# A second load buffer for stage D, and stages A and B one round earlier

## The chip, the cores and the metric

The kernel runs on one core of a Trainium2 chip. The metric is device time in microseconds (us) of one execution.

## The reference

```python
# x: [8, 3008, 256]; w_r, w_i: [256, 256]; w_in: [256, 2048]; w_out: [2048, 256]
X = np.fft.rfft(x, axis=1)                  # along the 3008 positions
Yr = X.real @ w_r - X.imag @ w_i + b_r
Yi = X.real @ w_i + X.imag @ w_r + b_i
Yr = np.sign(Yr) * np.maximum(np.abs(Yr) - 0.01, 0.0)
Yi = np.sign(Yi) * np.maximum(np.abs(Yi) - 0.01, 0.0)
y = np.fft.irfft(Yr + 1j * Yi, n=3008, axis=1).reshape(24064, 256)
h = np.maximum(y @ w_in, 0.0)
out = h * h @ w_out                         # [24064, 256]
```

## The kernel before

Two jobs run interleaved on all engines: the transform of a batch (stages A to D) and the two matrix products on the tokens of the batch before it.

**Products.** The tokens of a batch are cut into six chunks (`WIDTHS`, one of 470, four of 508, one of 506), 48 chunks in all. A chunk takes eight *rounds* (`NU`), one for each pair of 128 of the 2048 hidden features, so a batch takes a *cycle* of 48 rounds and the kernel 384 rounds and two to drain. In round r, TensorE (PE) runs the first product `mm1` into `ph`; ScalarE (ACT) applies two ReLUs (`g<-ph`) and a square (`g<-g`); VectorE (DVE) makes three sums (`sums`, L858 to L860). In round r+1 ScalarE makes a high part `gh` and VectorE a low part `gl` of these seven tiles, and in round r+2 PE runs the second product `mm2` of seven block products into `po`. Each product is three matmuls (`mm3`: high by high, high by low, low by high, profile lines L205 to L207). `ph` has one buffer: `mm1` of round r+1 waits for the two ReLUs of round r. After the second round of the next chunk (rounds 1, 9, 17, ... of a cycle) `put_together` copies and combines `po` with one ScalarE and seven VectorE operations (L876, L878 to L884); VectorE runs these during the round that follows (rounds 2, 10, 18, ..., 42), and `mm2` of that round writes `po` anew.

**Transform.** Stage A (13 groups, `plan_a`) loads `xin`, folds it on VectorE (`f`, L233 and L234), makes `fh` and `fl`, multiplies by a small table (`psa`), evicts to `eva` on ScalarE (L670) and stores to scratch memory in DRAM. Stage B and C (12 pairs, one every three rounds, `plan_b`): a load `bin`, points `psb`, copy `x`, its high and low parts `xh` and `xl` (L708), the mix by the weights (`psm`), bias, threshold, a turned copy `z`, its parts `zh` and `zl`, the way back (`psc`), eviction `evc` (L750) and a store to a second scratch. Stage D (13 groups, `plan_d`): a load `din`, points `psd` (L290), a copy `dv`, an unfolding on VectorE (`dx`, L297 and L298), and a high and a low part (L798, L802) into `xt`, the input of `mm1`.

**Order.** Nothing is scheduled by the compiler. Each step of a stage is registered with `at(round, place, do)`, and a round runs its places in a fixed order: load, `gh`, a1, `mm1`, p1, ReLUs and square, `gl`, v1, sums, `mm2`, p2, a2, v2, put-together. Steps at the same place run in the order in which they were registered. `stage_b[b]` is the round in which stage B of batch b begins; stage A begins 15 rounds earlier (`TURN`); `done[b]` is 41 rounds later. Stage D takes rounds in which stage B runs its points (`pair_round`) or in which there is no stage B. Every batch has two places where two stage D groups stand in rounds next to each other: its first two groups (rounds 45 and 46 of a cycle) and its third and fourth.

**Buffers and queue.** All transfers are issued by SyncE (SP) in order; one that waits for a buffer or for data holds all behind it. `din` has one buffer, `zh` one, `ld` (for `xin` and `bin`) two, `ev` (for `eva` and `evc`) two, the PSUM tag `f` of all small products two.

Of the kernel before, what the change touches and what calls it, by code (L numbers as in the profile page):

```python
# [45 lines left out]
GROUPS = [(g, min(W, N2 - g)) for g in range(0, N2, W)]  # L46
# [15 lines left out]
NCH = len(WIDTHS)  # L62
# [94 lines left out]
NU = NF // 2  # L157
# [7 lines left out]
def fft_mix_moe(ctx: ExitStack, tc: tile.TileContext, xp, xu, w_r, w_i, b_r, b_i,  # L165
                w_in, w_out, t_u, t_a, t_b, t_b0, t_m, t_d, sgn, outT):
    nc = tc.nc
    B = xp.shape[0] + xu.shape[0]
# [90 lines left out]
    nch = NCH * B  # L259
# [4 lines left out]
    def pieces(b, i):  # L264

        g, w = GROUPS[i]
        a, z = b * S + N1 * g, b * S + N1 * (g + w)
        out = []
        for c in range(NCH * b, NCH * (b + 1)):
            lo, hi = max(a, col0[c]), min(z, col0[c] + cols[c])  # L270
            if lo < hi:
                out.append((c, lo - col0[c], hi - lo, lo - a))
        return out

    def alloc_x(c):
        return [const.tile([P, 2, NCOL], F32R, tag=f"xt{k}", name=f"xt{k}", bufs=2) for k in range(2)]

    def load_d(b, i, t):
        g, w = GROUPS[i]
        nc.sync.dma_start(out=t[:NR * w], in_=scr2[b][:, g:g + w, :])  # L280

    def points_d(i, t, ps):
        g, w = GROUPS[i]
        n = NR * w
        tab = 0 if w == W else 2
        ps = ps[:, :4 * n].rearrange("p (k c m) -> p k c m", k=2, c=2)
        for part in range(2):
            for k in range(2):
                s = part * D + k * P
                nc.tensor.matmul(ps[:, k, part], t[:n, s:s + P], tD[:n, tab + part, :n],  # L290
                                 start=True, stop=True)
        return ps

    def unfold(i, ps, v, xf):
        w = GROUPS[i][1]
        n, m = NR * w, N1 * w
        nc.vector.tensor_add(xf[:, :, :n], ps[:, :, 0], v[:, :, :n])  # L297
        nc.vector.tensor_sub(xf[:, :, n:m], ps[:, :, 0, w:], v[:, :, w:n])  # L298
# [318 lines left out]
    def tl(tag, shape=(P, 512), dt=F32, bufs=1, name=None):  # L617
        return sb.tile(list(shape), dt, tag=tag, name=name or tag, bufs=bufs)

    def pst(name):  # L620
        return ps_f.tile([P, 512], F32, tag="f", name=name)
# [9 lines left out]
    def at(r, place, do):  # L631
        plan.setdefault((r, place), []).append(do)
# [5 lines left out]
    def plan_a(b, r0):  # L638
        for i, (g, w) in enumerate(GROUPS):
            def steps(i=i, n=NR * w, tab=0 if w == W else 2):  # L640
                s = {}

                def load():
                    if i == 0:
                        scratch1(b)
                    s["t"] = tl("ld", bufs=2, name="xin")[:n]
                    load_x(b, i, s["t"])

                def folded():
                    s["f"] = tl("ft", name="f")[:n]  # L650
                    fold(s["f"], s["t"])

                def high():
                    s["h"] = tl("fh", dt=F32R)[:n]
                    nc.scalar.copy(s["h"], s["f"])

                def low():
                    s["l"] = tl("fl", dt=F32R)[:n]
                    nc.vector.tensor_sub(s["l"], s["f"], s["h"].bitcast(F32))

                def points():
                    s["o"] = pst("psa")[:n]
                    for c in range(2):
                        cs = slice(c * D, c * D + D)
                        mm3(s["o"][:, cs], (tAs[0][:n, tab + c, :n], tAs[1][:n, tab + c, :n]),
                            (s["h"][:, cs], s["l"][:, cs]), True, True)

                def out():
                    e = tl("ev", bufs=2, name="eva")[:n]
                    nc.scalar.copy(e, s["o"])  # L670
                    store_a(b, i, e)

                r = r0 + i
                at(r - 2, "load", load)
                at(r, "v1", folded)
                at(r, "a2", high)
                at(r, "v2", low)
                at(r + 1, "p2", points)
                at(*((r + 2, "a1") if i + 1 < len(GROUPS) else (r + 1, "a2")), out)

            steps()
# [86 lines left out]

            steps()

    def plan_d(b, i, r):
        s = {}
        parts = pieces(b, i)

        def load():
            s["t"] = tl("din")
            load_d(b, i, s["t"])

        def points():
            s["ps"] = points_d(i, s["t"], pst("psd"))  # L780

        def take():
            s["v"] = tl("xh", (P, 3, 2, P), name="dv").rearrange("p a b m -> p (a b m)")
            s["v"] = s["v"][:, :2 * NR * W].rearrange("p (k m) -> p k m", k=2)
            nc.scalar.copy(s["v"][:, :, :s["ps"].shape[3]], s["ps"][:, :, 1])

        def unfolded():
            if len(parts) == 1:
                x = tl("xl", (P, 3, 2, P), name="dx").rearrange("p a b m -> p (a b m)")
            else:  # L790
                x = tl("o0", (P, 2, HALF), name="dx").rearrange("p a m -> p (a m)")
            s["x"] = x[:, :2 * N1 * W].rearrange("p (k m) -> p k m", k=2)
            unfold(i, s["ps"], s["v"], s["x"])

        def high(c, to, m, a):
            if c not in xts:
                xts[c] = alloc_x(c)
            nc.scalar.copy(xts[c][0][:, :, to:to + m], s["x"][:, :, a:a + m])  # L798

        def low(c, to, m, a):  # L800
            hi, lo = (x[:, :, to:to + m] for x in xts[c])
            nc.vector.tensor_sub(lo, s["x"][:, :, a:a + m], hi.bitcast(F32))  # L802

        at(max(r - 2, done.get(b, 0)), "load", load)
        at(r, "p1", points)
        at(r, "a2", take)
        at(r, "v2", unfolded)
        for k, part in enumerate(parts):

            q = NU * (part[0] - 1) if k else r + 1  # L810
            at(q, "a1", lambda part=part: high(*part))
            at(q, "v1", lambda part=part: low(*part))

    stage_b = {b: 3 + NU * NCH * (b - 1) for b in range(1, B)}

    done = {b: r + PAIR * (NPAIR - 1) + 8 for b, r in stage_b.items()}

    def pair_round(r):

        return all((r - r0) % PAIR == 0 for r0 in stage_b.values() if r0 <= r < r0 + PAIR * NPAIR)  # L820

    for b, r in stage_b.items():
        if b > 1:
            plan_a(b, r - TURN)
        plan_b(b, r)
    for c in range(1, nch):
        b = c // NCH
        rounds = [r for r in range(max(NU * (c - 1) - 1, 2), NU * c - 1) if pair_round(r)]
        units = [i for i in range(len(GROUPS)) if pieces(b, i)[0][0] == c]
        for i, r in zip(units, rounds[-len(units):]):  # L830
            assert r - 1 >= done.get(b, 0), (c, i, r)
            assert len(pieces(b, i)) == 1 or r >= NU * (c - 1) + 2, (c, i, r)
            plan_d(b, i, r)

    def mm1(c, j):
        n = cols[c]
# [55 lines left out]
    last = nch * NU  # L892
    with tc.manual_schedule():
        for r in range(last + LAG):
            c, j = divmod(r, NU)
# [68 lines left out]
```

## Time and profile before

| | |
|---|---|
| time, median of 3 runs | 2669.49 us (2668.97 to 2671.93) |
| profiled execution: time, span | 2671.44 us, 2669.7 us |
| busy: PE, DVE, ACT | 2583.5 us (97%), 2123.1 us (80%), 2014.2 us (75%) |
| TensorE clock granted, mean | 0.991 |
| first round begins | 143.9 us |

A busy time is the sum over an engine's instructions; idle time is put down to what ended it ("<-"). SPq is SP's queue of transfers, PEld the loading of weights on PE, which runs beside its matmuls. The first cycle ends near 466 us, and cycles 1 to 5 take about 322 us each; cycle 6 has no stage A, cycle 7 only stage D and products.

### The profile page before, as it was taken

To read this page: it belongs to the slowest core of one execution; us is meant where nothing else is said; L and a number is where in the kernel's file an instruction comes from. 1 tells how busy PE (TensorE), PEld (TensorE's weight loads), DVE (VectorE), ACT (ScalarE), POOL (GpSimd) and SP (SyncE) were. 2 spreads that over 40 slices of the span, in tenths; PEclk is the share of its full clock that TensorE was granted. 3 is DMA by queue.
4 is the path that set the end of the run, shared out by engine and by line. 5 is a ranking of instruction groups with operands and counts; after the bars stand their busy time and mean duration, and the time that the engine had idled before them with its cause. 6 is when DMAs were issued, how large, how long until landed. Compare 5 with 4: busy or idle time off the path is not lost.

```text
span 2669.7 us, 42564 instructions
## 1 busy us (share of the span) xinstructions
PE 2583.5 (97%) x16760; PEld 2328.8 (87%) x16760; DVE 2123.1 (80%) x3177; ACT 2014.2 (75%) x2785; POOL 50.9 (2%) x60
## 2 busy tenths in 40 slices
PE   6879999999999999999999999999999999999998
PEld 3579998999989999899988999899998999998887
DVE  5768888888888888888887888878888888877776
ACT  3667887777877887777877787777787778776765
POOL 1410000000000000000000000000000000000000
PEclk8989999999999999999999999999999999999999
DMA  9611113111132112311122111221113111110000
GB/s 264 196 39 48 46 54 97 47 58 40 54 92 61 40 47 64 104 40 42 36 87 86 39 40 58 83 71 39 51 50 92 55 54 48 31 34 25 22 25 16
DMA packets 127753, 165.16 MB, mean 62 GB/s; under 512 B 11184, under 2 KB 89762, under 8 KB 127362
## 3 DMA queue, kind: packets, MB, share of 16 engines
q1 hardware_dynamic: 127554, 162.44, 20.5%
q8 instruction: 133, 2.18, 0.3%
q14 instruction: 66, 0.54, 0.1%
HBM read 87.43 MB, written 74.97 MB: 61 GB/s over the span
## 4 chain that ended last, share of the span: by engine, by line
PE 61%; DVE 19%; ACT 12%; DMA 4%; issue 3%; POOL 1%; ACTq 0%; SPq 0%; DVEq 0%; POOLq 0%
PE ph L205 8%; PE ph L206 8%; PE ph L207 8%; PE po L205 7%; PE po L207 7%; PE po L206 7%; ACT gh L901 6%; DVE gl L909 5%; DVE g L858 3%; PE psb L242 3%; PE psm L207 2%; PE psd L290 2%; PE psm L205 2%; PE psm L206 2%; ACT g L852 2%
## 5 line engine op out<-in xcount | busy, mean ns | idle before, releaser
L909 DVE TENSOR_TENSOR gl<-g,gh 128x1778 fp32r<-128x1778 f32 (+1 forms) x384 | 763.6, 1989 | 332.9 <-ACT gh L901 332.9
L901 ACT CAST gh<-g 128x1778 fp32r<-128x1778 f32 (+1 forms) x384 | 638.7, 1663 | 381.7 <-DVE g L860 305.8
L205 PE MATMUL po<-gh,wo 128*128 128x254 f32 (+1 forms) x2688 | 764.8, 285 | 6.4 <-DVE o L878 3.6
L206 PE MATMUL po<-gl,wo 128*128 128x254 f32 (+1 forms) x2688 | 753.0, 280 | 2.6 <-DVE gl L909 2.6
L207 PE MATMUL po<-gh,wo 128*128 128x254 f32 (+1 forms) x2688 | 752.9, 280 | 0.0
L205 PE MATMUL ph<-xt,wi 128*128 128x508 f32 (+2 forms) x1536 | 608.6, 396 | 16.2 <-ACT xt L199 10.6
L206 PE MATMUL ph<-xt,wi 128*128 128x508 f32 (+2 forms) x1536 | 599.9, 391 | 1.8 <-DVE xt L802 1.7
L207 PE MATMUL ph<-xt,wi 128*128 128x508 f32 (+2 forms) x1536 | 599.0, 390 | 0.0
L205 PEld LDWEIGHTS po<-gh,wo 128*128 128x128 f32 x2688 | 509.4, 190 | 21.1 <-DVE o L878 7.7
L206 PEld LDWEIGHTS po<-gl,wo 128*128 128x128 f32 x2688 | 509.8, 190 | 10.7 <-DVE gl L909 3.0
L207 PEld LDWEIGHTS po<-gh,wo 128*128 128x128 f32 x2688 | 510.4, 190 | 0.0
L851 ACT ACTIVATE g<-ph 128x508 f32<-128x508 f32 (+1 forms) x768 | 410.4, 588 | 68.9 <-PE ph L207 67.7
L852 ACT ACTIVATE g<-g 128x1016 f32<-128x1016 f32 (+1 forms) x384 | 401.5, 1046 | 12.2
L205 PEld LDWEIGHTS ph<-xt,wi 128*128 128x128 f32 x1536 | 290.3, 189 | 66.8 <-ACT xt L199 10.9
L207 PEld LDWEIGHTS ph<-xt,wi 128*128 128x128 f32 x1536 | 290.2, 189 | 58.7
L206 PEld LDWEIGHTS ph<-xt,wi 128*128 128x128 f32 x1536 | 290.4, 189 | 48.7 <-DVE xt L802 3.7
L858 DVE TENSOR_TENSOR g<-g 128x508 f32<-128x508 f32 (+1 forms) x384 | 260.7, 679 | 46.1 <-ACT g L852 39.4
L859 DVE TENSOR_TENSOR g<-g 128x254 f32<-128x254 f32 (+1 forms) x384 | 161.6, 421 | 13.2
L860 DVE TENSOR_TENSOR g<-g 128x254 f32<-128x254 f32 (+1 forms) x384 | 161.5, 421 | 13.2
L207 PE MATMUL psm<-wm,xl 128*128 128x256 f32 (+1 forms) x552 | 161.6, 293 | 2.9 <-DVE xl L708 2.4
L205 PE MATMUL psm<-wm,xh 128*128 128x256 f32 (+1 forms) x552 | 160.9, 291 | 2.3 <-ACT eva L670 2.3
L206 PE MATMUL psm<-wm,xh 128*128 128x256 f32 (+1 forms) x552 | 159.1, 288 | 0.0
(107 smaller groups left out, 2765.4 us busy)
## 6 DMA issues: line engine op xcount, KB each, us to landing
bin<-s SPq DMA_DIRECT2D x96, 256.0 KB
s<-evc SPq DMA_DIRECT2D x96, 256.0 KB
din<-s SPq DMA_DIRECT2D x96, 240.0 KB
outT_dram<-o SPq DMA_DIRECT2D x144, 127.0 KB
xin<-in_xp_dram SPq DMA_DIRECT2D x72, 240.0 KB
s<-eva SPq DMA_DIRECT2D x72, 240.0 KB
s<-eva SPq DMA_DIRECT2D x22, 192.0 KB
w<-in_moe_w_in_dram SPq DMA_DIRECT2D x8, 512.0 KB
```

The costliest lines, as they stand in the source:

```text
L205: nc.tensor.matmul(out, l0, r0, start=start, stop=False, **kw)
L206: nc.tensor.matmul(out, l0, r1, start=False, stop=False, **kw)
L207: nc.tensor.matmul(out, l1, r0, start=False, stop=stop, **kw)
L242: nc.tensor.matmul(ps[:, k, :, q, :], tv[:, q, k], tB[:, 0:r + 2:r + 1], start=True, stop=True)
L290: nc.tensor.matmul(ps[:, k, part], t[:n, s:s + P], tD[:n, tab + part, :n], start=True, stop=True)
L851: nc.scalar.activation(g[:, t:4:2, :m], ph[:, :, t * t0:t * t0 + m], AF.Relu)
L852: nc.scalar.activation(g[:, 0:4, :m], g[:, 0:4, :m], AF.Square)
L858: nc.vector.tensor_sub(g[:, 4:6, :m], g[:, 1:4:2, :m], g[:, 0:2, :m])
L859: nc.vector.tensor_sub(g[:, 6, :m], g[:, 3, :m], g[:, 4, :m])
L860: nc.vector.tensor_sub(g[:, 1, :m], g[:, 6, :m], g[:, 2, :m])
L901: nc.scalar.copy(gg[k][0][:, :, :m], hid[k][:, :, :m])
L909: nc.vector.tensor_sub(gg[k][1][:, :, :m], hid.pop(k)[:, :, :m], gg[k][0][:, :, :m].bitcast(F32))
```

## The change

Three things change. Where two stage D groups stand in rounds next to each other, the second is loaded into the buffer of `zh`, the high operand of stage C, in place of `din`. Stage B of batches 2 to 7 begins one round sooner (rounds 2 and not 3 of a cycle), and with it stage A of these batches and `done`; the rounds of stage D follow by the rule above. And stage D is registered ahead of A and B, so that at each place it runs first.

```diff
-    def plan_d(b, i, r):
+    def plan_d(b, i, r, tag):
...
         def load():
-            s["t"] = tl("din")
+            s["t"] = tl(tag, name="din")
             load_d(b, i, s["t"])
...
-    stage_b = {b: 3 + NU * NCH * (b - 1) for b in range(1, B)}
+    stage_b = {b: (3 if b == 1 else 2) + NU * NCH * (b - 1) for b in range(1, B)}
...
+    for c in range(1, nch):
...
+        last = -2
+        for i, r in zip(units, rounds[-len(units):]):
...
+            plan_d(b, i, r, "zh" if r == last + 1 else "din")
+            last = r
     for b, r in stage_b.items():
         if b > 1:
             plan_a(b, r - TURN)
         plan_b(b, r)
-    for c in range(1, nch):
...
-            plan_d(b, i, r)
```

Rounds 45 and 46 of stage D stay. Its third and fourth group go from rounds 2 and 3 to 1 and 2, its fifth from 6 to 5, the later ones by one round back or two on.

SP, from stage A's load of round 43 of cycle 1 on (`s_2` is the second scratch of batch 2, `xin` a load of stage A, `eva` and `evc` stores). Before:

```order
L218 DMA xin<-in_xp_dram 120x512
L226 DMA s_3_6771<-eva 24x5x512
L230 DMA s_2_4555<-evc 128x2x256
L218 DMA xin<-in_xp_dram 120x512
L280 DMA din<-s_2_4555 120x1x512 x2
L226 DMA s_3_6771<-eva 24x5x512
L218 DMA xin<-in_xp_dram 120x512
L226 DMA s_3_6771<-eva 24x5x512
```

After:

```order
L218 DMA xin<-in_xp_dram 120x512
L226 DMA s_3_6702<-eva 24x5x512
L230 DMA s_2_4496<-evc 128x2x256
L280 DMA din<-s_2_4496 120x1x512
L218 DMA xin<-in_xp_dram 120x512
L226 DMA s_3_6702<-eva 24x5x512
L280 DMA din<-s_2_4496 120x1x512
L218 DMA xin<-in_xp_dram 120x512
```

The two `din` loads stood together behind a stage A load; now each stands ahead of one, with a store between them. The rows after the change are those of a round earlier.

ScalarE, round 42 of cycle 1, from the copy of the put-together (L876 before, L879 after) on. Before:

```order
L876 COPY o_7372<-po_6809 128x254
L901 CAST gh<-g 128x1778
L670 COPY eva<-psa 120x512
L851 ACTIVATE g<-ph 128x2x254 x2
L852 ACTIVATE g<-g 128x1016
L655 CAST fh<-f 120x512
L901 CAST gh<-g 128x1778
L670 COPY eva<-psa 120x512
L851 ACTIVATE g<-ph 128x2x254 x2
L852 ACTIVATE g<-g 128x1016
L750 COPY evc<-psc 128x512
```

After:

```order
L879 COPY o_7391<-po_6828 128x254
L904 CAST gh<-g 128x1778
L670 COPY eva<-psa 120x512
L854 ACTIVATE g<-ph 128x2x254 x2
L855 ACTIVATE g<-g 128x1016
L750 COPY evc<-psc 128x512
L655 CAST fh<-f 120x512
L904 CAST gh<-g 128x1778
L670 COPY eva<-psa 120x512
L854 ACTIVATE g<-ph 128x2x254 x2
L855 ACTIVATE g<-g 128x1016
```

The last `evc` of a batch moved from the round after the put-together's into its own.

VectorE, rounds 2 and 3 of cycle 1, from the put-together's last row (L884 before, L887 after) on. Before:

```order
L884 TENSOR_TENSOR o_4542<-o_4542,po_4029 128x254
L909 TENSOR_TENSOR gl<-g,gh 128x7x236
L858 TENSOR_TENSOR g<-g 128x2x236
L859 TENSOR_TENSOR g<-g 128x236
L860 TENSOR_TENSOR g<-g 128x236
L297 TENSOR_TENSOR dx<-psd,dv 128x2x120
L298 TENSOR_TENSOR dx<-psd,dv 128x2x115
L909 TENSOR_TENSOR gl<-g,gh 128x7x236
L802 TENSOR_TENSOR xt_4621<-dx,xt_4620 128x2x235
L858 TENSOR_TENSOR g<-g 128x2x236
L859 TENSOR_TENSOR g<-g 128x236
```

After:

```order
L887 TENSOR_TENSOR o_4555<-o_4555,po_4048 128x254
L912 TENSOR_TENSOR gl<-g,gh 128x7x236
L802 TENSOR_TENSOR xt_4572<-dx,xt_4571 128x2x235
L861 TENSOR_TENSOR g<-g 128x2x236
L862 TENSOR_TENSOR g<-g 128x236
L863 TENSOR_TENSOR g<-g 128x236
L297 TENSOR_TENSOR dx<-psd,dv 128x2x120
L298 TENSOR_TENSOR dx<-psd,dv 128x2x115
L912 TENSOR_TENSOR gl<-g,gh 128x7x236
L802 TENSOR_TENSOR xt_4572<-dx,xt_4571 128x2x235
L250 TENSOR_TENSOR x<-x 128x256
L861 TENSOR_TENSOR g<-g 128x2x236
```

The unfolding of stage D's third group (L297, L298) has gone ahead of the put-together, its split (L802) has come between the put-together's `gl` and the sums of round 2, and the unfolding behind them is now the fourth group's.

More of the change, by code (lines that the diff above doesn't have):

```diff
@@ L820, in pair_round @@
         return all((r - r0) % PAIR == 0 for r0 in stage_b.values() if r0 <= r < r0 + PAIR * NPAIR)
+    for c in range(1, nch):
+        b = c // NCH
+        rounds = [r for r in range(max(NU * (c - 1) - 1, 2), NU * c - 1) if pair_round(r)]
+        units = [i for i in range(len(GROUPS)) if pieces(b, i)[0][0] == c]
+        last = -2
+        for i, r in zip(units, rounds[-len(units):]):
+            assert r - 1 >= done.get(b, 0), (c, i, r)
+            assert len(pieces(b, i)) == 1 or r >= NU * (c - 1) + 2, (c, i, r)
+            plan_d(b, i, r, "zh" if r == last + 1 else "din")
+            last = r
     for b, r in stage_b.items():
@@ L825, in fft_mix_moe @@
         plan_b(b, r)
-    for c in range(1, nch):
[L827 to L832, printed above, removed]
-            plan_d(b, i, r)
     def mm1(c, j):
```

## The prediction

> **What bounds the kernel now.** I read the page first, then PE's waits in the steady stretch, then the timelines of SP, PE, VectorE and ScalarE around those waits. "Round k" is a round's place in its cycle of 48 rounds, six chunks, one batch; cycle 2 lies between 787 and 1109 us.
>
> ```profile
> PE 2583.5 (97%) x16760; PEld 2328.8 (87%) x16760; DVE 2123.1 (80%) x3177; ACT 2014.2 (75%) x2785; POOL 50.9 (2%) x60
> 0.00:144.00 144.00, 102.07 (x369) 61.91 (x369) 90.31 (x145) 72.13 (x137) 48.79 (x59) 0.88 0.74 218
> ```
>
> PE bounds it. Of its 86.2 us of idle time (2669.7 - 2583.5) 41.9 lie in the first 144 us, before the rounds begin, where the change touches nothing. What can be won lies in the rounds. PE's waits from 200 to 2150 us, columns total, times, longest:
>
> ```profile
> PE psd L290 <- DMA din<-s: 8.2, 6, 1.5
> PE psb L242 <- DMA bin<-s: 3.7, 2, 2.5
> PE po L205 <- DVE o L878: 3.6, 6, 0.7
> PE psm L207 <- DVE xl L708: 2.4, 7, 0.3
> ...
> PE psb L242 <- DVE g L859: 1.8, 2, 0.9
> PE ph L205 <- ACT g L851: 1.8, 5, 0.6
> ...
> PE psb L242 <- DVE g L860: 1.3, 1, 1.3
> PE psb L242 <- DVE g L858: 0.6, 1, 0.6
> ```
>
> Six waits for din and six for stage B's first points (psb, 7.4 us together under four names), one of each a cycle. SP's own rows, end of cycle 2 and start of cycle 3, show why:
>
> ```profile
> 1081.23 0.36 SPq L218 DMA_DIRECT2D xin<-in_xp_dram  x1
> 1081.69 0.75 SPq L226 DMA_DIRECT2D s<-eva  x1
> ...
> 1087.23 0.34 SPq L218 DMA_DIRECT2D xin<-in_xp_dram  x1
> 1087.67 5.82 SPq L280 DMA_DIRECT2D din<-s  x2
> ...
> 1106.57 0.78 SPq L280 DMA_DIRECT2D din<-s  x1
> 1123.67 0.76 SPq L280 DMA_DIRECT2D din<-s  x1
> 1124.53 1.58 SPq L226 DMA_DIRECT2D s<-eva  x2
> ...
> 1129.15 0.90 SPq L222 DMA_DIRECT2D bin<-s  x2
> ```
> ```profile
> 1091.55 0.70 PE L290 MATMUL psd<-tD,din 120*128 120x120 f32 x4 [1.42 <-DMA din<-s]
> 1131.42 0.28 PE L206 MATMUL po<-gl,wo 128*128 128x236 f32 x1
> 1131.53 0.27 PE L207 MATMUL po<-gh,wo 128*128 128x236 f32 x1
> 1132.69 1.13 PE L242 MATMUL psb<-tB,bin 128*128 128x128 f32 x8 [0.89 <-DVE g L859]
> ```
>
> SP works in order. The first din load of round 44 stands behind stage A's load, which waits for its buffer until 1087.23; issued at 1087.67 it lands for PE at 1091.55. So it is the first group of the pair that waits, and not the second. The second load of the other pair waits for the one din buffer until 1123.67; behind it stand two stores of stage A and then bin, issued at 1129.15 and needed at 1131.64 (one step of 0.11 after 1131.53; the wait is put down to VectorE, but bin's landing fits). Matmuls overlap: 0.28 long, 0.11 apart. So a wait costs its gap plus about 0.16.
>
> **The change part by part.** No instruction and no transfer is added or removed, and each keeps its shape, so every engine's busy time stays and all terms are waits.
>
> *din two rounds ahead and first on SP* (rounds 43 and 44 in place of 44). In cycles 1 to 5 the load precedes round 43's stage A load and waits only for the last stage C store; it is issued about a round sooner, against a wait of 1.4. Gone: 5 x (8.2/6 + 0.16) = 7.6. In cycle 0 stage B has not moved, the load stays in round 44, only ahead of stage A's: about 0.4 sooner, 0.4 gained. Together 8.0.
>
> *The second group in zh.* SP is not held from 1106.57 to 1123.67 any more, so stage A's last stores and bin go out as they are made. bin waits for the last of these stores. Its tile is evicted at the start of round 1 and the store lands some 4.3 later (rows below), bin at most 3.5 after that (1129.15 to 1132.69): 8 to 9 us. The points stand at the end of round 2, two rounds of over 5 away, so nothing is late. zh is free: stage C's last use is in round 42 (43 in cycle 0), its next in round 7. Gone: 7.4 + 6 x 0.16 = 8.4. Between them nobody else writes or reads zh.
>
> *Stages A and B a round sooner against the put-together*, VectorE's seven operations on po that stand in round 42, 2 and so on, every eight rounds. They do not move. Rounds 42, 43 and 44 of cycle 2 begin with PE's rows at 1066.87, 1074.24 and 1080.87:
>
> ```profile
> 1066.87 0.41 PE L205 MATMUL ph<-xt,wi 128*128 128x506 f32 x1
> 1069.98 0.42 DVE L878 TENSOR_TENSOR o<-po,o 128x254 f32<-128x254 f32 x1
> 1072.35 0.38 PE L205 MATMUL po<-gh,wo 128*128 128x254 f32 x1
> 1074.24 0.39 PE L205 MATMUL ph<-xt,wi 128*128 128x506 f32 x1
> 1074.79 0.42 DVE L234 TENSOR_TENSOR f<-xin 120x256 f32<-120x256 f32 x1
> 1080.79 0.42 DVE L234 TENSOR_TENSOR f<-xin 120x256 f32<-120x256 f32 x1
> 1080.87 0.39 PE L205 MATMUL ph<-xt,wi 128*128 128x506 f32 x1
> 1085.50 0.59 ACT L670 COPY eva<-psa 120x512 f32<-120x512 f32 x1 [1.01 <-DMA s<-eva]
> ```
>
> Gain: stage C's three matmuls (some 0.7: round 43, which has them, is 6.63 long) now precede round 42's second-layer matmuls, which today wait 0.6 for L878, plus 0.16, and once more some 0.3 (the row at 1072.35). Most of that goes: 5 x 0.9 = 4.5; 0.15 a cycle stays. With the din wait and its stage A store gone, the wait of ph for ScalarE in round 45 goes in the same cycles: 1.8 + 5 x 0.16 = 2.6.
>
> Loss: two buffers serve the evictions eva and evc. After an evc the next eva waits for the store of the eva before, which SP holds behind a stage A load, which waits for a fold on VectorE. Here the fold ended at 1081.21 and eva began at 1085.50, 4.3 later. Evc now falls into round 42, where the put-together makes the fold late: it ends 8.3 after the round's start (1075.21 - 1066.87), and 8.0 after the change, as sums run a little sooner. Round 42 will be about 6.75 long, so eva starts 1.25 + 4.3 = 5.55 into round 43, the two ReLUs behind it end 1.6 later, at 7.15 to 7.25, and that round has the work of round 43 today without stage C, 6.63 - 0.7 = 5.93. PE then waits some 1.3 for ph in round 44: 5 x 1.3 = 6.5. What hides it today is that evc comes a round after the put-together.
>
> By the Trainium skill, "DMA: Bandwidth & Descriptors", section "Anatomy of one DMA — SWDGE (gpsimd) path", a transfer takes about 2.0 us and its bytes over 436 GB/s: for 240 KB 2.6, an estimate from that page's fit for another issuing path. By it the loss in round 44 would shrink to about 0.1 and the sum grow to -14. The rows have 3.8 from issue to release (1081.69 to 1085.50), and the trace decides.
>
> *Stage B's first rounds.* Today the put-together of round 2 is followed by one stage D unfolding; afterwards round 2 has D's third group to be split, D's fourth group and B's first points. The nearest rows are rounds 10 and 11, and 19, of cycle 2, where a put-together is followed by a split of stage D (L802) and stage B's low part:
>
> ```profile
> 854.05 2.00 DVE L909 TENSOR_TENSOR gl<-g,gh 128x1778 fp32r<-128x1778 f32 x1
> 856.30 0.64 DVE L802 TENSOR_TENSOR xt<-dx,xt 128x470 fp32r<-128x470 f32 x1
> 858.37 0.95 DVE L708 TENSOR_TENSOR xl<-x,xh 128x768 fp32r<-128x768 f32 x1
> ```
> ```profile
> 858.77 0.28 PE L206 MATMUL psm<-wm,xh 128*128 128x256 f32 x1
> 859.38 0.38 PE L207 MATMUL psm<-wm,xl 128*128 128x256 f32 x1 [0.33 <-DVE xl L708]
> 910.56 0.47 PE L205 MATMUL ph<-xt,wi 128*128 128x508 f32 x1
> 915.24 1.08 ACT L851 ACTIVATE g<-ph 128x508 f32<-128x508 f32 x2
> 1133.58 0.47 PE L205 MATMUL ph<-xt,wi 128*128 128x470 f32 x1
> 1138.58 0.38 PE L205 MATMUL ph<-xt,wi 128*128 128x470 f32 x1
> ```
>
> In round 19 the ReLUs end 5.76 after the round's start (915.24 + 1.08 - 910.56). The round after B's first points, round 3 afterwards, has no extra PE work and is 5.0 long (1133.58 to 1138.58). ReLUs as late there, with D's split ahead of B's copy on ScalarE, leave PE waiting 0.8 for ph at the start of round 4, and xl, 0.5 late in round 11 (859.38 against 858.77 + 0.12), is late by 0.6 in B's first mix. With 0.1 on po: 1.5 x 6 = 9.0. Bounds: 0, if VectorE catches up, and 2.9 + 0.6 + 1.0 (seven put-together operations of 0.42, L802, L708) = 4.5 a cycle.
>
> The waits of psm in round 11 move to round 19 and those of round 19 to round 27: nothing. Stage D ahead of A and B at each place changes no sum elsewhere.
>
> Sum: -8.0 - 8.4 - 4.5 - 2.6 + 6.5 + 9.0 = **-8.0**. It is made on the profiled execution (span 2669.7, time 2671.4); the median of the runs, 2669.5, is 2 lower, and the same 8 off it give **2661.5 us**.
>
> **Rivals.** (1) The waits go and the losses do not come: -8 - 15.5, so 2646; with only the loss of rounds 3 and 4 missing 2652.5. For it: PE waits for ScalarE's ReLUs only five times in the whole stretch. Against: xl and the ReLUs are late in rounds 11 and 19, where stage D follows the put-together today. (2) The store of stage A lands within 2.5, because fewer loads run beside it, and only the loss of round 44 is missing: 2655. Against: the store's 3.8 and din's 3.9 (1087.67 to 1091.55) in the rows. This is the case in which the page of the Trainium skill named above would be right. (3) All is handed back: the losses grow by half, or din still waits, for its wait belongs to the first group, which the second buffer does not touch: 2667 to 2672, the same. For it: evc, the put-together and the late store meet in one round, where VectorE and ScalarE wait for each other. Against: stage A's load now stands behind din. (4) Slower: in rounds 2 to 4 put-together, split and xl land whole on PE's path, 4.5 a cycle in place of 1.5: +18, 2679.5. It decides from (8 + 5.3) / 6 = 2.2 more a cycle. Against: the one like place in the trace lost 0.5.
>
> **How the numbers follow.** Forecast 0.50 (2657 to 2666), rival 1 and its half 0.14, rival 2 0.07, rival 3 0.22, rival 4 0.07. 0.2%, 5.3 us, is about what a measurement of this kernel can tell from no change, so faster means under 2664.2: 0.44 of the forecast and rivals 1 and 2, 0.65. Same is the rest of the forecast and rival 3, 0.28; slower 0.07. The range for 8 in 10 goes from 2651, below rivals 2 and the half of 1, to 2669, into rival 3.
>
> **What would show it.** In the changed profile PE's wait for din shrinks to one (cycle 0), psb waits vanish, L878 waits shrink below 0.2. New: PE ph waiting for ScalarE in rounds 44 and 4, L207 psm for xl in round 4, and still twelve waits of eva for its store. SP shows no hold of over 5 us for psd before bin. Wrong would be: ph does not wait in rounds 44 and 4, or din still waits in every cycle.

## The result and the profile after

The changed kernel takes 2656.61 us (median of six runs, 2654.18 to 2657.63) against 2670.71 us before (six runs): ratio 0.9945, 95% interval 0.9935 to 0.9956, so 11.8 to 17.4 us less. The forecast was 2661.5 us, with a range of 2651 to 2669. The two profiled executions differ by 17.3 us of span (2669.7 and 2652.4).

The page's engine line after, and PE's waits from 200 to 2150 us (total, times, longest):

```profile
PE 2579.0 (97%) x16760; PEld 2329.7 (88%) x16760; DVE 2117.2 (80%) x3177; ACT 2006.1 (76%) x2785; POOL 51.1 (2%) x60
PE ph L205 <- ACT g L854: 8.5, 11, 1.7
PE psm L205 <- ACT eva L670: 4.0, 5, 0.8
PE psm L207 <- DVE xl L708: 2.1, 6, 0.4
PE psa L205 <- DVE dx L298: 1.6, 1, 1.6
PE psa L205 <- DVE e L256: 1.5, 6, 0.3
PE po L205 <- DVE o L881: 0.6, 1, 0.6
PE psc L205 <- ACT x L246: 0.4, 1, 0.4
```

Each engine has as many instructions as before; the busy times fell by 4.5, 5.9 and 8.1 us (PE, DVE, ACT), where the prediction had them unchanged.

No wait for din or bin is left, in cycle 0 neither. ph now waits for ScalarE eleven times, five of them in round 44. That place, cycle 2: SP, then ScalarE, VectorE and PE.

```profile
1070.01 0.38 SPq L218 DMA_DIRECT2D xin<-in_xp_dram  x1
1070.49 0.79 SPq L226 DMA_DIRECT2D s<-eva  x1
1071.38 0.47 SPq L230 DMA_DIRECT2D s<-evc  x1
1075.73 0.78 SPq L280 DMA_DIRECT2D din<-s  x1
1076.61 0.50 SPq L218 DMA_DIRECT2D xin<-in_xp_dram  x1
```
```profile
1068.45 0.56 ACT L750 COPY evc<-psc 128x512 f32<-128x512 f32 x1
1069.56 0.42 DVE L234 TENSOR_TENSOR f<-xin 120x256 f32<-120x256 f32 x1
1075.05 0.59 ACT L670 COPY eva<-psa 120x512 f32<-120x512 f32 x1 [1.79 <-DMA s<-eva]
1075.53 1.09 ACT L854 ACTIVATE g<-ph 128x508 f32<-128x508 f32 x2
1076.67 0.50 PE L205 MATMUL ph<-xt,wi 128*128 128x506 f32 x1 [1.57 <-ACT g L854]
```

This is the forecast chain row by row: evc takes a buffer in the put-together's round, the fold ends at 1069.98 and lets stage A's load go, the eva store behind it is issued at 1070.49 and releases the next eva at 1075.05, and the ReLUs behind that hold PE for 1.57. din, at 1075.73, now goes ahead of the next stage A load. In the five cycles the wait was 0.66 to 1.74, mean 1.28; forecast 1.3. The store needed 4.6 us to its release (1075.05 - 1070.49). By the rule of the Trainium skill weighed in the prediction ("DMA: Bandwidth & Descriptors", "Anatomy of one DMA — SWDGE (gpsimd) path"; 2.6 as an estimate for 240 KB, from a fit for another issuing path) this wait would hardly exist; the measurement decides against it here.

Behind the longest of the five waits, in cycle 5, the granted clock fell as well: PE's row, and the window that follows (the column with 0.50 is PE's granted clock).

```profile
2034.14 0.49 PE L205 MATMUL ph<-xt,wi 128*128 128x506 f32 x1 [1.74 <-ACT g L854]
2035.10:2038.50 3.40, 3.40 (x9) 2.67 (x9) 2.13 (x4) 2.18 (x4) 0.00 (x0) 0.50 0.77 218
```

In this window the matmuls of ph come 0.42 apart, at full clock 0.23: eight of them took 1.5 us more. The table below counts the wait and not this.

Round 4 of cycle 3, PE:

```profile
1126.18 0.48 PE L205 MATMUL ph<-xt,wi 128*128 128x470 f32 x1 [0.36 <-ACT g L854]
1129.64 0.39 PE L207 MATMUL psm<-wm,xl 128*128 128x256 f32 x1 [0.39 <-DVE xl L708]
```

Both waits that were forecast stand there, at half and at two thirds of their forecast size. For all places together I took, for each of PE's matmuls, the time from its start to the next start beyond the median for its kind in the profile before, and summed this by place over the eight cycles (us, before to after):

| place | change | forecast |
|---|---|---|
| round 45, psd for din | 9.2 to 0: -9.2 | -8.0 |
| round 3, psb | 8.3 to 0: -8.3 | -8.4 |
| round 42, po for L878 | 6.7 to 2.3: -4.4 | -4.5 |
| round 45, ph | 3.0 to 0.4: -2.6 | -2.6 |
| round 44, ph | 0 to 7.6: +7.6 | +6.5 |
| round 4, ph and psm for xl | 0 to 6.0: +6.0 | +9.0 |
| round 11, psm for xl; round 19, psc | 3.5 and 1.6 to 0: -5.1 | 0 |
| psm for eva: round 38, now 37 | 3.3 to 4.8: +1.5 | 0 |
| rounds 36 and 37 of cycle 0, psa and psc | 0 to 2.4: +2.4 | 0 |
| sum | -12.1 | -8.0 |

Of the other 5.2 us, 1.4 lie ahead of round 3, which PE begins at 162.3 before and at 160.9 after; from the first round to there the granted clock was 0.80 and 0.90. Another 1.3 lie in the last stretch (last section). Nothing in the profiles puts either down to the change. What is left is spread thin.

### The profile page after: what moved, and what is told of

The parts are those of the page before. It is cut to its first block, busy times and chain, and to the rows that moved or that the text cites. A ratio compares the mean times of both kernels' runs of the same rounds, so it can differ in the third digit from the quotient of the medians.

```text
span 2652.4 us, 42581 instructions
## 1 busy us (share of the span) xinstructions
PE 2579.0 (97%) x16760; PEld 2329.7 (88%) x16760; DVE 2117.2 (80%) x3177; ACT 2006.1 (76%) x2785; POOL 51.1 (2%) x60
## 4 chain that ended last, share of the span: by engine, by line
PE 54%; DVE 21%; ACT 17%; issue 4%; DMA 3%; POOL 1%; SPq 0%; ACTq 0%; DVEq 0%; POOLq 0%
ACT gh L904 8%; PE ph L206 7%; PE ph L205 7%; PE ph L207 7%; PE po L205 6%; PE po L207 6%; PE po L206 6%; DVE gl L912 5%; DVE g L861 4%; ACT g L854 3%; ACT g L855 3%; PE psb L242 3%; DVE g L862 2%; DMA s<-eva 2%; PE psm L207 2%
```

## Experiments

All ratios are to the kernel before, run beside it, with 95% intervals. The first four kernels ran on one chip and split the change in its parts. "A and B a round sooner" without "stage D first" was not tried. PE's waits are those from 200 to 2150 us throughout.

**e1, zh alone.** `plan_d(b, i, r, "zh" if r == last + 1 else "din")`, all else as before.

> Against the kernel before, only the buffer changes: the second of two neighbouring stage D groups is loaded into zh; stages A and B and the order of registration stay. Theory (the waits are separate, as in the prediction): SP is no longer held for the one din buffer, so the psb wait of round 3 goes (8.3 us over the six cycles), while the din wait of round 45 (9.2 us) stays, since it belongs to the first group, whose load stands behind stage A's load. Ratio to before 0.9969 (-8.3 us). Rival 1, the two din waits have one cause, two loads for one buffer: both go, -17.5 us, ratio 0.9934. Rival 2, the wait is handed on to the next thing that is late in round 3: ratio 0.999 to 1.000.

Measured 2664.64 us, ratio 0.9970 (0.9961 to 0.9980), as the theory has it. The psb wait is gone, and the first group of the pair still waits for din, 10.4 us in six waits: two waits, two causes.

**e2, stage D first alone.**

```diff
+    for c in range(1, nch):
+        ...plan_d(b, i, r, "din")
     for b, r in stage_b.items():
         ...plan_a, plan_b
-    for c in range(1, nch):
-        ...plan_d(b, i, r)
```

> Against the kernel before, only the order of registration changes: stage D's steps run first at each place. One din buffer, stages A and B where they were. Theory a (the prediction's step): stage D's first load only passes one stage A load and goes out some 0.4 us sooner, against a wait of 1.4; gain 0.4 x 6 = 2.4 us, ratio 0.9991, and the din wait of round 45 stays at about 1 us. Theory b (what cycle 0 of the changed profile suggests, where stage B has not moved and yet no din wait is left): the order on SP alone takes the whole wait, -9.2 us, ratio 0.9966. In both the psb wait of round 3 stays, since the second load still holds SP. Rival: stage D first on ScalarE and VectorE makes stage C's or stage A's steps late, as in rounds 36 and 37 of cycle 0 of the changed profile (2.4 us): up to 14 us back, ratio 1.002.

Measured 2648.46 us, ratio 0.9908 (0.9894 to 0.9921): more than any theory gave, and faster than the whole change. Theory a fell: no wait for din is left. What the rest is, e5, e6 and e12 take apart.

**e3, zh and stage D first, stages A and B where they were.** The changed kernel with `stage_b = {b: 3 + NU * NCH * (b - 1) ...}`.

> The change without its middle part: second group in zh and stage D first at each place, but stages A and B of all batches where they were before. Theory b: psb wait and din wait both go (8.3 + 9.2), the waits for L878 in round 42 (6.7) stay, and neither the wait of ph in round 44 (8) nor those of round 4 (6) come, since evc stays a round behind the put-together and stage B's points a round behind it: -17.5 us, ratio 0.9934, some 3 us below the changed kernel; moving stages A and B a round sooner was then no gain. Theory a: the din wait stays at 1 us a cycle, -11 us, ratio 0.996. Rival: the stage D order costs as in cycle 0 of the changed profile, 2.4 us a cycle: -3 us, ratio 0.999.

Measured 2645.91 us, ratio 0.9899 (0.9883 to 0.9915). The changed kernel lies at 0.9945: moving stages A and B a round sooner cost about 12 us, 0.0046 with an interval of some 0.0019 to both sides. Beside e2, zh gives 0.0009, which can't be told from nothing. The profiles of e2 and e3 show a part of the reason: in e2 psb waits 5.8 us in round 3, in e3 not at all, but there psm waits 1.8 us for xl in round 5, where e2 has no wait.

They also show which of the table's waits belong to moving A and B. Neither e2 nor e3 has a wait of psm for eva, so the order alone took the 3.3 us of round 38, and the 4.8 of round 37 came with the move; the 2.4 us in rounds 36 and 37 of cycle 0 are in neither as well.

**e4, the change without zh** (tag `"din"` for all).

> The change without its first part: one din buffer for all groups of stage D, stages A and B a round sooner and stage D first as in the changed kernel. Theory: the second load of the pair in rounds 1 and 2 again holds SP until the first group's points have run, with stage A's last stores and bin behind it, so psb waits again, now in round 2 (6 x 1.4 = 8.3 us), and the rest is as in the changed kernel: -14.5 + 8.3 = -6.2 us, ratio 0.9977. Rival: the held queue costs nothing now, because the losses of rounds 3 and 4 would take the time anyway (bin late by 1.4 and ReLUs late by 0.5 overlap): ratio 0.9945 to 0.996.

Measured 2658.01 us, ratio 0.9938 (0.9925 to 0.9952), level with the changed kernel, as the rival has it. The expected 8.3 us did not come: SP is still held for the one din buffer, but psb waits only 2.3 us in all, and ph in round 44 5.6 and not 7.6. Against e2 on the same chip, A and B sooner cost 0.0030.

**e5, only stage D's loads first**, in the kernel before.

```diff
+    FIRST = ("load",)
+    def at_d(r, place, do):    # for all steps of plan_d
+        # ahead of A's and B's steps where place is in FIRST, else as at()
```

> Against the kernel before, only SP's order changes: stage D's loads go first at their place, all other steps of stage D stay behind those of A and B; one din buffer, A and B where they were. Theory (the gain of e2 has two causes): the din load of round 44 goes out when the last stage C store has landed, some 1.3 us sooner than behind stage A's load, and the din wait goes, 9.2 us, and nothing else; the waits of psm for xl (round 11, 3.5), of psc (round 19, 1.6) and of psm for eva (round 38, 3.3) stay as before: ratio 0.9966. Rival: all of e2's gain comes through SP's queue, by loads that land earlier everywhere: ratio 0.991.

Measured 2663.20 us, ratio 0.9966 (0.9953 to 0.9978), the theory's number. SP, end of cycle 2, and two of PE's waits:

```profile
1079.00 0.36 SPq L218 DMA_DIRECT2D xin<-in_xp_dram  x1
1079.46 0.75 SPq L226 DMA_DIRECT2D s<-eva  x1
1080.31 0.47 SPq L230 DMA_DIRECT2D s<-evc  x1
1084.05 5.58 SPq L280 DMA_DIRECT2D din<-s  x2
```
```profile
PE psd L290 <- DVE dx L298: 2.6, 6, 0.5
PE psm L207 <- DVE xl L719: 2.3, 7, 0.3
```

din goes 5.05 after the stage A load of the round before (1084.05 - 1079.00), where it went 6.44 after it (1087.67 - 1081.23): 1.4 sooner, as long as the wait was. It now waits only for the evc store to land. The second group of the pair waits instead, in round 46, 0.4 to 0.5 each, and psm's wait for xl stays. The theory had neither this new wait (3.6 us with what follows each) nor 2.0 us less at psb; they partly cancel.

**e6, only stage D's copy dv (a2) and unfolding (v2) first**: `FIRST = ("a2", "v2")`.

> Against the kernel before, only stage D's copy dv on ScalarE (place a2) and its unfolding on VectorE (place v2) go ahead of those of A and B; its loads, splits and all else stay. Theory: dv now runs in a gap in which ScalarE waited for VectorE's e, so ScalarE and VectorE reach gh and gl 0.3 to 0.7 us earlier in rounds 10, 11, 18, 19, 37 and 38, and the waits of psm for xl, of psc and of psm for eva go (3.5 + 1.6 + 3.3 = 8.4 us), while the din wait (9.2) and the psb wait (8.3) stay: ratio 0.9969. Rival 1, these places change no sum (the prediction's step): ratio 1.000. Rival 2: dv ahead makes stage C's turned copy or stage A's fh late and gives half of it back: ratio 0.9985.

Measured 2658.73 us, ratio 0.9949 (0.9936 to 0.9963), 5 us more than the theory's sum. All of PE's waits that are left:

```profile
PE psd L290 <- DMA din<-s: 7.6, 6, 1.5
PE psb L242 <- DMA bin<-s: 5.9, 6, 1.0
PE po L205 <- DVE o L892: 3.2, 6, 0.7
PE ph L205 <- ACT g L865: 2.2, 6, 0.6
PE psa L205 <- DVE e L256: 1.6, 6, 0.3
```

psm's waits for xl and eva are gone and psc's too, 8.4 us as expected; psb lost another 1.5, din 0.6, and 2.6 us went in steps too small for a place. ScalarE and VectorE of the kernel before, end of round 9 and start of round 10 of cycle 2, show what stood in the way:

```profile
848.52 0.41 ACT L732 COPY z<-e 64x256 f32<-64x256 f32 x1 [0.35 <-DVE e L724]
...
849.88 0.50 ACT L733 ACTIVATE z<-e,sg 64x256 f32<-64x256 f32 x1
850.40 0.36 ACT L785 COPY dv<-psd 128x240 f32<-128x240 f32 x1
...
851.05 1.68 ACT L901 CAST gh<-g 128x1778 fp32r<-128x1778 f32 x1
...
850.80 0.41 DVE L297 TENSOR_TENSOR dx<-psd,dv 128x240 f32<-128x240 f32 x1 [0.79 <-ACT dv L785]
```

The same place in e2, where the whole of stage D is first:

```profile
840.49 0.34 ACT L785 COPY dv<-psd 128x240 f32<-128x240 f32 x1
840.94 0.41 ACT L732 COPY z<-e 64x256 f32<-64x256 f32 x1
...
842.29 0.51 ACT L733 ACTIVATE z<-e,sg 64x256 f32<-64x256 f32 x1
...
843.20 1.68 ACT L904 CAST gh<-g 128x1778 fp32r<-128x1778 f32 x1
...
842.34 0.40 DVE L297 TENSOR_TENSOR dx<-psd,dv 128x240 f32<-128x240 f32 x1
```

Before, ScalarE stood idle for VectorE's e (the mixed product with its bias and threshold; 0.35), did the four copies of z, and only then dv, for which VectorE waited 0.79. Put first, dv fills the idle time. Counted from the last copy of z, gh starts 0.91 later and not 1.17, and the unfolding 0.05 later and not 0.92; behind the unfolding stand the put-together, gl and xl.

**e12, only dv first**: `FIRST = ("a2",)`.

> Against the kernel before, only stage D's copy dv on ScalarE goes ahead of stage A's and B's steps at its place; its unfolding, loads and splits stay behind. Theory: in round 10 the unfolding had waited 0.79 us for this copy and not for VectorE's order, so the copy alone does what e6 did: ratio 0.995 as e6 (psm for xl, psc and psm for eva gone, din and psb left). Rival: the order on VectorE (unfolding ahead of stage A's fl in round 37) is the half of it, and psm's wait for eva in round 38 stays: 0.9965.

Measured 2660.42 us, ratio 0.9961 (0.9947 to 0.9974). The waits of psm and psc are gone as in e6, which speaks for the copy alone; the time lies between theory and rival, and its interval reaches to both, and to e6. The unfolding alone ahead, and the places p1, a1 and v1 alone, were not tried; e5 and e6 together give 0.0085 of e2's 0.0092.

**e7, the changed kernel with the last evc of a batch elsewhere.**

```diff
-    e = tl("ev", bufs=2, name="evc")
+    e = tl("ev", bufs=2, name="evc") if i + 1 < NPAIR else tl("z", name="evc")
```

> The changed kernel with one edit: the last evc of each batch goes into the buffer of z, which is free by then, and not into one of the two buffers it shares with eva. Theory (the prediction's loss term): the wait of ph for ScalarE in round 44 comes from eva that waits for its store because evc took a buffer in the put-together's round; with evc elsewhere the wait of eva for its store and that of ph go, 7.6 + 1 us: ratio to before 0.9945 - 0.0030 = 0.9915. Rival: ph waits because ScalarE has evc, the put-together's copy and gh in one round; then nothing changes, 0.9945. A second rival: half goes, as something else is nearly as late: 0.993.

Measured 2647.14 us, ratio 0.9908 (0.9894 to 0.9922). ScalarE's waits for the store, and PE's for ScalarE:

```profile
ACT eva L670 <- DMA s<-eva: 4.9, 7, 1.6
PE ph L205 <- ACT g L854: 2.2, 6, 0.6
```

The wait of ph in round 44 is gone, and it was the store. evc still runs in the put-together's round, so ScalarE's load there was not the cause.

**e8, e3 with the last evc in z.**

> e3 (second group in zh, stage D first, A and B where they were) with the last evc of each batch in the buffer of z. Theory: in e3 eva waits 1.64 us for its store in round 44, and ph 0.6 to 0.8 in round 45 behind it; with evc elsewhere this wait goes, 4.1 us over the run: ratio 0.990 - 0.0015 = 0.9885. Rival: something else in round 44 is as late (gh at 1.9 after the round's start): 0.990.

Measured 2642.20 us, ratio 0.9885 (0.9871 to 0.9899). PE's waits, all of them:

```profile
PE po L205 <- DVE o L881: 3.7, 6, 0.7
PE psd L290 <- DMA din<-s: 1.6, 4, 0.5
PE psa L205 <- DVE e L256: 1.5, 6, 0.3
```

The ratio is the theory's, and the wait of ph in round 45 (2.9 us in e3) is gone; a wait for din (1.6) has come. The gain over e3, 0.0014, is within the intervals of the two.

**e9, e7 with stage D's third and fourth group in rounds 0 and 1.**

```diff
+    if c % NCH == 1 and c > 1:
+        rounds = [r - 1 for r in rounds[:2]] + rounds[2:]
```

> e7 (the changed kernel with the last evc in z) with one more edit: in every cycle from the second on the third and fourth group of stage D stand in rounds 0 and 1, not 1 and 2, so that the put-together of round 2 is followed by one split and no unfolding of stage D. Theory (the prediction's second loss): the waits of round 4, ph for ScalarE (2.8 us) and psm for xl (3.1), come from the unfolding and the split that stand between the put-together and stage B's first pair; both go, -5.9 us: ratio 0.9908 - 0.0022 = 0.9886. Rival 1: the put-together alone makes round 3 late, nothing changes, 0.9908. Rival 2: the load of the third group stands a round sooner behind those of rounds 44 and 45, and psd waits for it in round 0, or stage A's last steps in rounds 0 and 1 are late: half or all is given back, 0.9898 to 0.9915.

Measured 2648.99 us, ratio 0.9916 (0.9902 to 0.9929): no gain over e7. At round 4 ph lost half its excess (2.8 to 1.4), psm's wait for xl stayed (3.1), and as much came back elsewhere in small steps. That does not clear stage D. In e9 the fourth group's split (L798, L802) has left round 3, but it now stands in round 2 where the third's was, between the put-together's gl and the sums. In cycle 3 of e9, xl starts 7.74 us after the start of round 3, in e7 7.96 after it; but PE, no longer held at ph, begins round 4 after 5.28 us and not after 5.51, and so waits for xl just as long. What makes ScalarE and VectorE late there, the put-together or the split behind it, no run tells apart.

**e10, e9 with stage A's first eva half a round sooner**: `if 0 < i < len(GROUPS) - 1 else (r + 1, "a2")`.

> e9 with one more edit: stage A's first group of each batch is evicted (eva) a half round sooner, at the end of the round in which it is multiplied and not behind zh in the next. Theory: psm waits in round 37 for this eva, because it holds one of the two small PSUM buffers (5.1 us in e7, from 3.3 in the kernel before, where it stood in round 38); that wait goes: 0.0018 below e9's ratio, and the moved stages A and B, freed of all three waits that they brought, are then level with or below e8 (0.9885). Rival: eva ahead of gh makes gh late by its 0.58 us, and PE waits as long elsewhere: the ratio of e9.

Measured 2651.84 us, ratio 0.9920 (0.9907 to 0.9934). Miss: psm's wait for eva is gone from round 37, and psa now waits there for e instead, which holds the other small PSUM buffers:

```profile
PE psa L205 <- DVE e L256: 7.5, 6, 1.5
```

**e11, e8 with the last pair's psc and evc a round sooner.**

```diff
-    at(r + 7, "p1", back)
-    at(r + 7, "a2", out)
+    k = r + 7 if i + 1 < NPAIR else r + 6
+    at(k, "p1", back)
+    at(k, "a2", out)
```

> e8 (second group in zh, stage D first, A and B where they were, last evc in z) with one more edit: the way back psc and evc of the last pair of each batch stand in round 42 (43 in the first cycle's numbering no different), one round sooner; nothing else of stages A to C moves. Theory: this takes from the moved stages only what they gave, the three matmuls ahead of round 42's second product, which waits for L881 (7.0 us in e8, about 2.5 where stages A and B were moved), and an earlier last store, so that psd no longer waits for din (2.8): -7 us, ratio 0.9885 - 0.0027 = 0.9858. Rival: evc in the put-together's round makes ScalarE late, and ph waits in round 43 as long as is saved: 0.9885.

Measured 2639.25 us, ratio 0.9884 (0.9871 to 0.9898): both waits went as expected (7.0 to 2.2 in round 42, 2.8 to 0 for din), and the time is that of e8. Of the 7.6 us, 3.3 came back in round 5 of the cycles, far from the edit, and 1.7 in small steps; the 2.6 left would not show in an interval of 0.0014 (3.7 us). VectorE and PE in round 5 of cycle 3, e11:

```profile
1126.12 0.95 DVE L708 TENSOR_TENSOR xl<-x,xh 128x768 fp32r<-128x768 f32 x1
1126.35 0.28 PE L205 MATMUL psm<-wm,xh 128*128 128x256 f32 x1
1127.12 0.39 PE L207 MATMUL psm<-wm,xl 128*128 128x256 f32 x1 [0.38 <-DVE xl L708]
```

and in e8:

```profile
1125.49 0.95 DVE L708 TENSOR_TENSOR xl<-x,xh 128x768 fp32r<-128x768 f32 x1
1126.61 0.28 PE L205 MATMUL psm<-wm,xh 128*128 128x256 f32 x1
```

In e8 xl starts 1.12 ahead of PE's first mix, in e11 0.23. VectorE is no slower: from the start of the gl before it to that of xl it takes 4.36 us in e11 and 4.35 in e8. PE lost less time in rounds 42 and 45 and comes to round 5 some 0.9 further ahead of VectorE. e8 and e11 have the lowest medians of all, 1.2% below the kernel before and 0.6% below the changed one; e3, at 0.9899, is not clear of them.

## Why the prediction was right, and where it was wrong

The kernel became faster by more than 0.2%, and its time lies inside the range; the gain was 14.1 us by the medians where 8 were forecast. Point by point:

- *Second group in zh* (-8.4): psb lost 8.3, and e1 shows it alone at -8. But beside the other two parts zh is worth nothing that can be measured (e4 against the changed kernel, e2 against e3). The step's price was right for the kernel before; once stage D came first, what psb lost was lost at other places instead (psm for xl in e3).
- *din two rounds ahead and first on SP* (-8.0): -9.2. The failed step is cycle 0, where "only ahead of stage A's: about 0.4 sooner" was forecast. I counted the passed load's own time and not the wait at its head: SP stood there until a fold was done. e5 puts it at 1.4 sooner, the whole wait, by order alone. The round that the prediction held for the cause was not needed.
- *Gains of A and B a round sooner* (-4.5 and -2.6): -4.4 and -2.6.
- *Loss in round 44* (+6.5): +7.6, and e7 shows its cause, the shared eviction buffer and the late store. The wait itself was 1.28 where 1.3 was forecast; the term left out the 0.16 that a wait costs above its gap, and the fall of the granted clock behind one of them (1.5 us). Rival 2 fell.
- *Loss in rounds 3 and 4* (+9.0): mis-sized, +6.0. ph waited 0.36 a cycle and not 0.8, xl 0.39 and not 0.6, in five cycles and hardly in the sixth, and po not at all. Its cause as I gave it, stage D's split and unfolding behind the put-together, holds at best for half of ph (e9); for xl it stays open, as in e9 one split still stands there.
- "*Stage D ahead of A and B at each place changes no sum elsewhere*": wrong, and the largest error. Against the kernel before, the order of dv and the unfolding alone is worth 0.0051 (e6), beside 0.0034 for the loads (e5). I looked at sums and not at what ScalarE waits for at the head of a place.
- "*The waits of psm in round 11 move to round 19 and those of round 19 to round 27*": wrong, they ceased, in e2 and e3 without any move of the rounds.
- Put at nothing without a reason: the wait of psm for eva that the move brings in round 37 (4.8), and the waits of rounds 36 and 37 of cycle 0, where A moves and B does not (2.4).

So that the time fell into the range is in part luck, for large errors of opposite sign cancelled. Taken one after the other, the three parts of the change stand in the sum as follows, with the din gain of cycles 1 to 5 counted to the move, whose round the prediction held for its cause (us; measured from the ratios of e2, e3 and the changed kernel, each good to some 4 to 6 us):

| part | forecast | measured |
|---|---|---|
| stage D first | -0.4 | -24.6 |
| second group in zh | -8.4 | -2.4 |
| A and B a round sooner (-7.6 - 4.5 - 2.6 + 6.5 + 9.0) | +0.8 | +12.3 |
| together | -8.0 | -14.7 |

## What to carry to other kernels

On engines that work in order, ask at each place not only what stands there but also which instruction at its head waits: work that is ready, put ahead of it, fills the idle time for nothing, and one line of registration order gave here what a buffer and a shifted plan did not. Run each part of a change alone and the whole without each part; here one part carried the gain, one was redundant beside it and one cost. And when a second pair of engines runs close behind the bound, a wait taken from the bound comes back where that pair is latest, so count a gain only after looking a whole cycle on.

## What the runs showed of the hardware

PE's last stretch is the same work in both kernels, twenty matmuls after a wait of 1.66 and 1.67 us. The profile before, by windows (PEclk is the column with 0.59), and its first matmuls there:

```profile
2660.00:2664.02 4.02, 3.69 (x19) 3.69 (x20) 1.54 (x4) 0.37 (x1) 0.00 (x0) 0.59 0.10 32
2660.92 0.42 PE L205 MATMUL po<-gh,wo 128*128 128x254 f32 x1
2661.13 0.42 PE L206 MATMUL po<-gl,wo 128*128 128x254 f32 x1
```

and after:

```profile
2644.00:2647.00 3.00, 2.44 (x20) 2.43 (x20) 1.61 (x4) 0.37 (x1) 0.00 (x0) 1.00 0.00 0
2644.89 0.28 PE L205 MATMUL po<-gh,wo 128*128 128x254 f32 x1
2645.01 0.28 PE L206 MATMUL po<-gl,wo 128*128 128x254 f32 x1
```

Before, the granted clock fell (0.59 is the mean of the window) and most of the matmuls came 0.21 apart; after, it stayed at 1.00 and they came 0.12 apart. From the first of the twenty to the last it is 3.69 us before (2660.33 to 2664.02) and 2.36 after (2644.55 to 2646.91): 1.3 us that come of the clock, behind equal waits.

It also falls within the rounds, for 3.4 us at a time and to 0.50: once in the profile after, behind the wait of 1.74 in round 44 shown above, and twice in that of e12, from 1451.70 (behind a wait of psb of 2.13) and from 2052.40 (behind one of psd of 1.68). It did not fall behind the longest wait of psb in the profile before, 2.47. So a wait of PE can cost more than its gap, and not each time.

The Trainium skill, "TensorE: Matmul & The Clock Gate", Part 1, has a gate that halves the clock after an idle window and whose window runs free of the kernel, which would make the same waits end either way. These profiles agree that equal waits can end either way. The page has that window at about 3.4 us; no wait ahead of a fall in the rounds was as long (2.13 at most), so it did not take a window without any work here. No run tests what it takes.
